# A place of its own for local attention's result, and an earlier split of the output weights

## The chip, the cores and the metric

The kernel runs on one core of a Trainium2 chip. The metric is the device time of one execution in microseconds, as the median of several executions. A core has five engines that run their own instruction streams and wait for each other by semaphores: TensorE (PE, matrix products; PEld is its loading of weights), VectorE (DVE), ScalarE (ACT), GpSimd (POOL) and SyncE (SP), which here issues nearly all transfers (DMA).

## The reference

Two attentions over the same input `x` (2048 rows, 448 columns, 16 heads of 28) are computed and mixed by a gate of each row:

```python
g = sigmoid((x * gate_w).sum(-1, keepdims=True))
# A: local; row s sees rows s, s-2, ..., s-14 (8 of them), masked below row 0
#    softmax over the 8 logits, then @ A_wo
# B: all 2048 rows; softmax(q k^T * 28**-0.5) v, then @ B_wo
out = g * A(x) + (1 - g) * B(x)
```

## The kernel before, in words

**Stages.** First come the projections to q, k and v of both attentions. Then follows a main loop of 256 steps, `st = 16 u + kt`: 16 units `u` (a group of four heads g = u // 4 and a block of 512 queries b = u % 4) times 16 tiles `kt` of 128 keys. A step computes the scores of four heads (L1039, twelve products into three PSUM tiles T), two exponentials on ACT (L1042) and, for the step before, the products with V into `av` (L993). Since the softmax of full attention needs the maxima of its rows beforehand, PE also computes up to three score tiles a step for a later unit (`s1_mm`, L144), and DVE reduces them (`s1_max`, L148). These run ahead, and the last ones are in step 234; then `s1_close` frees their PSUM banks for the output product.

**What runs beside the loop.** Local attention is done by POOL and DVE, in eight columns `c` of two heads: products with k, reductions, softmax, products with v (`a_av`, L664 and L669 into `oat`). A column's result, `oats[c % 2]`, is turned by DVE (`a_turn`, L675, into `oatT`) and stored to `oa_scr` in DRAM (`a_store`, L681, eight DMAs). These pieces stand in four lists (pool, dve, act, sp) with costs and needed lags in steps; `issue` takes from each list what fits into a step. Other work is put at a step and a place in it by `at(place, step, f)`, with the places pre, mid, dve, act and end in that order. Each engine's program order is the order in which the steps write its instructions; nothing is reordered at run time, so an instruction that waits holds back everything behind it on its engine. SP's DMAs wait in the same way.

**The end of a unit.** When unit u is through, in step 16(u + 1) + 1 its `av` is copied by ACT (`fin_copy`, L849, `osb`). Its sums go to DRAM and back (`fin_sum`, `fin_sum2`, L854 and L858), DVE takes reciprocals and POOL multiplies them by one minus the gate (`fin_inv`, L862 and L863, `finv`), SP stores them (`fin_spread`, L867) and loads them back broadcast (`fin_spread2`, L872, `rbc`). POOL multiplies (`fin_on`, L901), ACT and POOL split into a high and a low part (`fin_hi` L905, `fin_lo` L909), and SP stores both (`fin_store`, L101). For unit 13 these are at the steps 225, 226, 230 (reciprocal and store), 231, 233, 236, 237 and 239; for unit 12 fin_lo is in step 224 and fin_store in step 227.

**The output product.** It has seven chunks of 128 rows: the 448 rows of local attention (chunks 0 to 2 and half of 3), then the 448 of full attention. Every product is done in three terms of high and low parts (`op_mm`, L833). Its weights `wo` are loaded raw into `rawt` in steps 200 and 202, and split by POOL (`split_wo`, L774 and L775, once per chunk). The tiles of `wo` get the place of local attention's tiles: `load_wo` closes those pools and opens new ones, and the first write into the new tiles waits for all that still reads or writes the old ones. `a_done` does it once all four lists are empty, which is so in step 225; the splits are put at the steps 226 to 229. Then the turned rows of block 0 are loaded into `rawt` (`op_load_a(0)`, L795, step 230) and split (`op_split`, L806 to L809: the high part of block 0 on DVE, of other blocks on ACT, the low part on DVE). The high and low rows of full attention come from DRAM (`op_load_b`, tiles `on`).

The output product goes through a queue of 92 items (`op_queue`): for row tiles j = 0 to 7 seven chunks and a copy out, for j = 8 to 11 six chunks and a copy of the partial sum (`part`). From step `OPS[0]` on, each step takes five of them. OPS is set in step 234 to `st + 3`, step 237. When tile j = 4b + 2 begins, the rows of block b + 1 are split. What is left is done after the loop, together with unit 15's end.

Of the kernel before, what the change touches and what calls it, by code (L numbers as in the profile page):

```python
# [8 lines left out]
F32 = mybir.dt.float32  # L9
F32R = mybir.dt.float32r  # L10
AF = mybir.ActivationFunctionType
ALU = mybir.AluOpType
# [3 lines left out]
S, D, H, DH = 2048, 448, 16, 28  # L16
NB, NJ, NG = 4, 16, 4
# [8 lines left out]
def gated_mix_kernel(ctx: ExitStack, tc: tile.TileContext, xT, xn, gw, wA, wB, woAB, out):  # L26
    nc = tc.nc
# [51 lines left out]
    QP = [[cp.tile([128, 512], F32R, name=f"QP{i}{k}") for k in range(2)] for i in range(2)]  # L79
# [126 lines left out]
    with tc.tile_pool(name="xp", bufs=1) as xp, tc.tile_pool(name="wp", bufs=2) as wp:  # L206
# [203 lines left out]
        r, t = xst[:, 0, 0:3, :], xst[:, 0, 3, :]  # L410
# [7 lines left out]
        for kt in range(3):  # L418
            nc.vector.tensor_tensor(out=xl[0][:, kt, :], in0=r[:, kt, :], in1=xh[0][:, kt, :].bitcast(F32),
                                    op=ALU.subtract)  # L420
        nc.vector.tensor_tensor(out=tail[64:128], in0=t[64:128], in1=tail[64:128].bitcast(F32), op=ALU.subtract)
        nc.vector.tensor_tensor(out=wl0[:, 3, 0:256], in0=wt0[:, 0:256], in1=wh0[:, 3, 0:256].bitcast(F32),
                                op=ALU.subtract)
# [27 lines left out]
        for n, t in enumerate(tiles):  # L451
# [4 lines left out]
            for w in splits:  # L456
                i, k = (n - splits[w][0]) * splits[w][1], splits[w][1]
# [36 lines left out]
            if parts and parts[0][0] <= n:  # L494
                _, u, t = parts.pop(0)
# [4 lines left out]
            if n == 64:  # L500
                gate = []
                for sgn, dst in ((-1.0, g_t), (1.0, omg)):
                    e = sp.tile([128, NJ], F32, name="ez")
# [5 lines left out]
            if n == 70:  # L509
                r = max_turn(omw)  # L510
# [10 lines left out]
    def at(pos, st, f):  # L521
        hooks.setdefault((st, pos), []).append(f)
# [12 lines left out]
    pool = ctx.enter_context(tc.tile_pool(name="psv", bufs=1, space=bass.MemoryType.PSUM))  # L535
# [38 lines left out]
    ep = ctx.enter_context(tc.tile_pool(name="ep", bufs=1))  # L574
# [9 lines left out]
        nc.gpsimd.memset(maskt[0:1, w, 0:DIL * w, :], -1e9 / SCALE)  # L584


    actx = ExitStack()
    a1 = actx.enter_context(tc.tile_pool(name="a1", bufs=1))
    a2 = actx.enter_context(tc.tile_pool(name="a2", bufs=2))
    a3 = actx.enter_context(tc.tile_pool(name="a3", bufs=5))  # L590
    kvt = {}
    oats = [a1.tile([128, NJ, 2, 32], F32, name=f"oat{i}") for i in range(2)]
    for t in oats:
        nc.gpsimd.memset(t, 0.0)  # L594
    for nme in ("k", "v"):
        for i in range(2):
            t = a1.tile([128, HALO + NJ, 56], F32, name=f"{nme}t{i}")
            kvt[nme, i] = t
    qt, Lt, oat, lst, prods = {}, {}, {}, {}, {}
# [69 lines left out]
            nc.gpsimd.tensor_tensor(out=oat[c], in0=oat[c], in1=oat[c, w], op=ALU.add)  # L669

    def a_turn(c, i):
        if i == 0:
            oaTt[c] = a1.tile([128, NJ, 2, 32], F32, name="oatT")
        r = slice(4 * i, 4 * i + 4)
        nc.vector.transpose(oaTt[c][:, r].rearrange("p j h e -> p (j h e)"),  # L675
                            oats[c % 2][:, r].rearrange("p j h e -> p (j h e)"))

    def a_store(c, a):
        for h in range(2):
            f = 56 * c + DH * h  # L680
            nc.sync.dma_start(oa_scr[f:f + DH].rearrange("f (j p) -> f j p", j=NJ)[:, :, 32 * a:32 * a + 32],  # L681
                              oaTt[c][32 * a:32 * a + DH, :, h, :])

    oaTt = {}


    lists = {"pool": [], "dve": [], "act": [], "sp": []}
# [84 lines left out]
    def split_wo(k):  # L772
        raw = rawt[:, D * k:D * k + D]
        nc.gpsimd.tensor_copy(wo[0][:, k, :], raw)  # L774
        nc.gpsimd.tensor_tensor(out=wo[1][:, k, :], in0=raw, in1=wo[0][:, k, :].bitcast(F32), op=ALU.subtract)  # L775
# [4 lines left out]
    def a_done(st):  # L780
        adone.append(st)
        load_wo()

        for i, k in enumerate((4, 5, 6, 0, 1, 2, 3)):
            at("act", st + 1 + i // 2, lambda k=k: split_wo(k))
        at("end", st + 5, lambda: op_load_a(0))

    oaT, onT = {}, {}

    def op_load_a(b):  # L790
        cs = slice(512 * b, 512 * b + 512)
        for k in range(4):
            n = 128 if k < 3 else 64
            raws[b, k] = rawt[0:n, 512 * k:512 * k + 512]
            nc.sync.dma_start(raws[b, k], oa_scr[128 * k:128 * k + n, cs])  # L795

    def op_split(b, k):
        if k < 3:
            i = (6 * b + 2 * k) % 12
            oaT[b, k] = [spare[x // 4][:, 512 * (x % 4):512 * (x % 4) + 512] for x in (i, i + 1)]  # L800
        else:
            oaT[b, k] = on_tiles(b)[0]
        raw = raws.pop((b, k))
        hi, lo = (t[0:128 if k < 3 else 64, :] for t in oaT[b, k])
        if b:
            nc.scalar.activation(hi, raw, AF.Copy)  # L806
        else:
            nc.vector.tensor_copy(hi, raw)
        nc.vector.tensor_tensor(out=lo, in0=raw, in1=hi.bitcast(F32), op=ALU.subtract)  # L809

    raws = {}
    spare = KH[1], KH[2], KL[0]
# [1 line left out]
    def on_tiles(b):  # L814
        if b not in onT:
            onT[b] = [[oP["2"].tile([128, 512], F32R, tag=f"on{p}{k}", name=f"on{p}{k}") for p in ("hi", "lo")]
                      for k in range(4)]
        return onT[b]

    def op_load_b(b, k, rows=128):  # L820
# [7 lines left out]
    def op_mm(j, bank, ks, first=False, last=False):  # L828
        b, jj = divmod(j, 4)
        for k in ks:  # L830
            for i, (a, c) in enumerate(TERMS):
                src = (oaT[b, k] if k < 3 else onT[b][k - 3])[a][:, 128 * jj:128 * jj + 128]
                writes(bank, nc.tensor.matmul(bank[:, :D], src, wo[c][:, k, :],  # L833
                                              start=(first and k == ks[0] and i == 0),
                                              stop=(last and k == ks[-1] and i == 2)))

    def op_out(j, bank, eng=0):
        t = mtile("res")
        if eng:
            reads(bank, nc.vector.tensor_copy(t[:, :D], bank[:, :D]))  # L840
        else:
            reads(bank, nc.scalar.activation(t[:, :D], bank[:, :D], AF.Copy))
        nc.sync.dma_start(out.rearrange("(p j) c -> p j c", j=NJ)[:, j, :], t[:, :D])
# [103 lines left out]


    def op_part(j, bank):
        part[j] = oP["1"].tile([128, D], F32, name=f"part{j}")  # L950
        reads(bank, nc.scalar.activation(part[j], bank[:, :D], AF.Copy))

    def op_rest(j, bank):
# [7 lines left out]
    def op_queue(j):  # L961
        bank = accs[j % 2]
        b = j // 4
        if j == 0:
            ks = (4, 5, 6, 0, 1, 2, 3)
            return [(0, lambda k=k: op_mm(j, bank, (k,), first=k == 4, last=k == 3)) for k in ks] + [
                (0, lambda: op_out(j, bank))]
        return [
            (0, lambda: op_mm(j, bank, (0,), first=True)),
            (0, lambda: op_mm(j, bank, (1,))),  # L970
            (0, lambda: op_mm(j, bank, (2,))),
            (READY[b, 0], lambda: op_mm(j, bank, (3,))),
            (READY[b, 1], lambda: op_mm(j, bank, (4,))),
            (READY[b, 2], lambda: op_mm(j, bank, (5,), last=b == 2)),
        ] + ([(0, lambda: op_part(j, bank))] if b == 2 else [
            (READY[b, 3], lambda: op_mm(j, bank, (6,), last=True)),
            (0, lambda: op_out(j, bank)),
        ])
# [97 lines left out]
    for u in range(NU):  # L1076
        g, b = divmod(u, NB)
        for kt in range(NJ):
            st = NJ * u + kt
            if kt == (8 if u < 12 else 12) and u + 1 < NU:  # L1080
                load_q(u + 1)
            run("pre", st)
            issue("sp", st, 0)
            if st >= A_START:
                issue("pool", st, 4.2)
            if not adone and not any(lists.values()):
                a_done(st)
            cur = {}
            left = s1e - s1c[0]
            for a in scores(u, kt, cur):  # L1090
                if a == 2:
                    run("mid", st)
            run("dve", st)
            if u and kt == 6:
                late["dve"] += 0.25
            if finished:
                v = finished.pop(0)
                t = max_parts(v)
                late["dve"] += 0.3
                late["pool"] += 0.18  # L1100
                turned = {}
                lag = 2 if v < NU - 1 else 1
                at("dve", st + lag, lambda t=t, w=turned: w.update(r=max_turn(t.bitcast(F32))))
                at("end", st + lag, lambda v=v, w=turned: max_store(v, w["r"]))
            issue("dve", st, DLIM)
            issue("act", st, 0)
            run("act", st)
            if prev is not None:
                do_av(prev)
            else:  # L1110
                for _ in range(2):
                    nc.tensor.matmul(av, KH[0][:, 0:128], KH[0][:, 0:512], start=True, stop=True, skip_group_check=True)
            prev = (kt, cur, g)
            if OPS and st >= OPS[0]:
                op_some(st, 5)
            run("end", st)
            step = 2.25 if left else 2.1
            late["dve"] = max(0.0, late["dve"] + 0.58 * min(3, left) - step)
            late["pool"] = max(0.0, late["pool"] - step)
            if st == OP0 + 31:  # L1120
                op_load_b(2, 3)
            if not OPS and s1c[0] == s1e:
                s1_close()
                for k in range(4):
                    at("act", st + 1 + k // 2, lambda k=k: op_split(0, k))
                OPS.append(st + 3)
    do_av(prev)
    fin_copy(15)
    while opj[0] < 12 or opq:
# [52 lines left out]
```

## Time and profile before

| | |
|---|---|
| median of 3 runs | 915.58 us (914.75 to 916.93) |
| the profiled execution | 915.27 us, its span 913.4 us |
| busy: PE, DVE, ACT, POOL | 900.1, 740.7, 645.9, 626.4 us |
| mean granted TensorE clock | 0.996 |
| POOL's seven splits of the output weights | first at 772.1 us, 0.56 + 1.15 us each |
| first product of the output (L833) | 799.6 us |

A profile's span runs from the first to the last instruction; the execution's own time has 1.9 us around it. In rows of the timeline the columns are start (us from the span's start), duration, engine, line, operation, what is written from what, and in brackets the idle time of the engine just before and what ended it. A row with a count merges several instructions, and its duration is from the first start to the last end.

### The profile page before, as it was taken

What the parts mean: (1) busy time and instruction counts of PE and PEld (TensorE: products, weight loads), DVE (VectorE), ACT (ScalarE), POOL (GpSimd) and SP (SyncE); (2) the same over time, 40 slices, a digit from 0 to 9 for tenths busy, and PEclk for the clock granted to TensorE, in tenths of its full rate; (3) what the DMA queues carried; (4) which work ended last, traced back from release to release, by engine and by line L of the source; (5) the groups of instructions that cost most, each with busy time, mean ns of one, the idle gap of its engine ahead of it and who ended that gap; (6) DMA issues with size and microseconds to landing.
All of it is one profiled execution on the core that took longest, in us unless ns stands there. A gap on an engine that the chain in (4) does not pass through costs nothing.

```text
span 913.4 us, 20598 instructions
## 1 busy us (share of the span) xinstructions
PE 900.1 (99%) x8334; PEld 530.2 (58%) x8334; DVE 740.7 (81%) x997; ACT 645.9 (71%) x775; POOL 626.4 (69%) x494
## 2 busy tenths in 40 slices
PE   9999999999999999999999999999999999799998
PEld 6889999999944444444444444444444444266667
DVE  6488999999989998999999999999999988510112
ACT  6456434343378888888988888888989888644550
POOL 2499846564479799998989999899998294400100
PEclk9999999999999999999999999999999999899999
DMA  9977403554373331344244322522222422454323
GB/s 266 295 258 201 129 11 94 156 128 113 82 244 94 94 99 45 93 104 120 46 120 123 101 82 58 131 90 63 73 57 63 108 50 40 144 176 130 96 91 102
DMA packets 113839, 104.30 MB, mean 114 GB/s; under 512 B 74628, under 2 KB 82180, under 8 KB 112960
## 3 DMA queue, kind: packets, MB, share of 16 engines
q1 hardware_dynamic: 113600, 102.72, 39.3%
q8 instruction: 65, 1.06, 0.5%
q10 hardware_dynamic: 144, 0.26, 0.1%
q14 instruction: 30, 0.25, 0.1%
HBM read 61.99 MB, written 40.48 MB: 112 GB/s over the span
## 4 chain that ended last, share of the span: by engine, by line
PE 94%; ACT 2%; POOL 2%; DMA 1%; SPq 1%; DVE 1%; issue 0%; ACTq 0%; POOLq 0%; DVEq 0%
PE T L1039 29%; PE av L993 27%; PE r L298 15%; PE T L833 8%; PE r L293 7%; PE r L144 4%; PE T L144 4%; ACT P L1042 1%; POOL wo L775 1%; DMA V<-in_xT 1%; DMA rbc<-rs 0%; POOL wo L774 0%; DVE MX L148 0%; SPq L795 0%; POOL oat L594 0%
## 5 line engine op out<-in xcount | busy, mean ns | idle before, releaser
L1042 ACT ACTIVATE P<-T 128x1024 f32<-128x1024 f32 x512 | 497.4, 1025 | 96.1 <-PE T L1039 94.3
L148 DVE TENSOR_REDUCE MX<-T 128x1 f32<-128x512 f32 x470 | 440.3, 952 | 22.4 <-PE T L144 10.3
L993 PE MATMUL av<-P,V 128*32 128x512 f32 x2048 | 273.6, 606 | 1.1 <-ACT osb L849 0.8
L1039 PEld LDWEIGHTS T<-QH,KH 30*128 30x128 f32 x1024 | 91.1, 182 | 228.1 <-ACT P L1042 205.4
L144 PE MATMUL T<-KH,QP 28*128 28x512 f32 x704 | 219.4, 454 | 0.3 <-DVE MX L162 0.3
L1039 PE MATMUL T<-QH,KH 30*128 30x512 f32 x1024 | 212.2, 490 | 6.2 <-ACT P L1042 5.8
L162 DVE TENSOR_REDUCE MX<-r 128x2 f32<-128x1024 f32 x160 | 192.6, 1221 | 24.7 <-PE r L144 23.1
L1039 PE MATMUL T<-QH,KL 28*128 28x512 f32 x1024 | 186.5, 397 | 0.0
L1039 PE MATMUL T<-QL,KH 28*128 28x512 f32 x1024 | 184.0, 394 | 0.0
L615 POOL TENSOR_TENSOR prod<-qt,kt 128x896 f32<-128x896 f32 x64 | 135.2, 2115 | 0.2
L362 ACT ACTIVATE raw<-r 128x896 f32<-128x896 f32 (+1 forms) x64 | 58.9, 921 | 97.9 <-PE r L298 96.6
L669 POOL TENSOR_TENSOR oat<-oat,prod 128x896 f32<-128x896 f32 x56 | 118.2, 2111 | 2.7
L144 PEld LDWEIGHTS T<-KH,QP 28*128 28x128 f32 x704 | 86.0, 181 | 27.7 <-ACT P L1042 21.4
L664 POOL TENSOR_TENSOR prod<-vt,L 128x896 f32<-128x896 f32 x56 | 95.5, 1705 | 0.5
L363 POOL TENSOR_TENSOR ast<-raw 128x448 f32<-128x448 f32 x48 | 55.4, 1155 | 58.1 <-ACT raw L362 45.7
L1039 PEld LDWEIGHTS T<-QL,KH 28*128 28x128 f32 x1024 | 93.6, 185 | 0.0
L1039 PEld LDWEIGHTS T<-QH,KL 28*128 28x128 f32 x1024 | 92.4, 183 | 1.0
L993 PEld LDWEIGHTS av<-P,V 128*32 128x32 f32 x2048 | 40.3, 108 | 79.1 <-issue 72.5
L298 PE MATMUL r<-wh,xh 64*128 64x448 f32 (+1 forms) x512 | 83.5, 362 | 0.0
L144 PE MATMUL r<-KH,QP 64*128 64x512 f32 x320 | 83.1, 390 | 0.0
L298 PE MATMUL r<-wh,xl 64*128 64x448 f32 (+1 forms) x384 | 69.4, 363 | 0.0
L298 PE MATMUL r<-wl,xh 64*128 64x448 f32 (+1 forms) x448 | 64.8, 367 | 0.0
(116 smaller groups left out, 1031.7 us busy)
## 6 DMA issues: line engine op xcount, KB each, us to landing
a_scr<-ast SPq DMA_DIRECT2D x24, 448.0 KB
qk_hi<-qkh SPq DMA_DIRECT2D x24, 256.0 KB
qk_lo<-qkh SPq DMA_DIRECT2D x24, 256.0 KB
rbc<-rs SPq DMA_DIRECT2D x60, 64.0 KB
QP<-qk_hi SPq DMA_DIRECT2D x64, 56.0 KB
KL<-qk_lo SPq DMA_DIRECT2D x16, 224.0 KB
QH<-qk_hi SPq DMA_DIRECT2D x64, 56.0 KB
QL<-qk_lo SPq DMA_DIRECT2D x64, 56.0 KB
```

The source lines that it names most:

```text
L144: nc.tensor.matmul(bank, qhis[u][h % 2][r, 128 * qs:128 * qs + 128], KH[u // NB % 3][r, 512 * kc:512 * kc + 512], start=True, stop=True)
L148: r = nc.vector.tensor_reduce(MX[:, n % NMX:n % NMX + k], bank, axis=X, op=ALU.max)
L162: nc.vector.tensor_reduce(m, PM[k], axis=X, op=ALU.max)
L293: nc.tensor.matmul(bank, ws[c][rows, k, t[4]:t[4] + 128], x, start=first, stop=last)
L298: nc.tensor.matmul(bank[:, 0:cols], x, ws[c][rows, k, 0:cols], start=first, stop=last)
L615: nc.gpsimd.tensor_tensor(out=p, in0=qt[c], in1=kvt["k", c % 2][:, HALO - DIL * w:HALO - DIL * w + NJ, :], op=ALU.mult)
L664: nc.gpsimd.tensor_tensor(out=dst, in0=kvt["v", c % 2][:, HALO - DIL * w:HALO - DIL * w + NJ, :].rearrange("p j (h d) -> p j h d", d=DH), ...
L669: nc.gpsimd.tensor_tensor(out=oat[c], in0=oat[c], in1=oat[c, w], op=ALU.add)
L833: writes(bank, nc.tensor.matmul(bank[:, :D], src, wo[c][:, k, :], start=(first and k == ks[0] and i == 0), stop=(last and k == ks[-1] and ...
L993: nc.tensor.matmul(av[32 * h:32 * h + 32, :], V[:, kt, 4 * g + h, :], tiles_[h], start=(kt == 0), stop=(kt == NJ - 1), skip_group_check=True)
L1039: nc.tensor.matmul(bank[a], (KH[g % 3], KH[g % 3], KL[g % 2])[t][r, ks], (qh, ql, qh)[t][r, :], start=(t == 0), stop=(t == 2))
L1042: e = nc.scalar.activation(p, RP[0] if a == "2" else mine, AF.Exp, scale=SCALE).ins
```

## The change

`oats` and `oatT` move from a pool of local attention to the pool `ep`, which stays open. `a_done` is now called when POOL's list alone is empty, in step 221, and one chunk of the weights is split in each of the steps 221 to 227, in the order 0 to 6. When all lists are empty, in step 225, a new function `a_stored` puts `op_load_a(0)` at step 229 and the splits of block 0's turned rows at the steps 232, 232, 233 and 234. For block 0 both halves of that split are now POOL's. The output queue starts two steps after the last row maximum (step 236), and its first tile takes the chunks in the order 0 to 6 like the others. The fourth pair of `on` tiles is now the pair `QP[b % 2]` of the row-maximum products, and the partial sums of tiles 8 to 11 lie in `oats`.

```diff
+    oats = [ep.tile([128, NJ, 2, 32], F32, name=f"oat{i}") for i in range(2)]
+    oatT = ep.tile([128, NJ, 2, 32], F32, name="oatT")
+    for t in oats:
+        nc.gpsimd.memset(t, 0.0)
...
-    oats = [a1.tile([128, NJ, 2, 32], F32, name=f"oat{i}") for i in range(2)]
-    for t in oats:
-        nc.gpsimd.memset(t, 0.0)
...
     def a_turn(c, i):
-        if i == 0:
-            oaTt[c] = a1.tile([128, NJ, 2, 32], F32, name="oatT")
...
-        for i, k in enumerate((4, 5, 6, 0, 1, 2, 3)):
-            at("act", st + 1 + i // 2, lambda k=k: split_wo(k))
-        at("end", st + 5, lambda: op_load_a(0))
+        for k in range(7):
+            at("act", st + k, lambda k=k: split_wo(k))
+
+    def a_stored(st):
+        adone.append(st)
+        at("end", st + 4, lambda: op_load_a(0))
+        for k, i in enumerate((7, 7, 8, 9)):
+            at("act", st + i, lambda k=k: op_split(0, k))
...
-            nc.vector.tensor_copy(hi, raw)
-        nc.vector.tensor_tensor(out=lo, in0=raw, in1=hi.bitcast(F32), op=ALU.subtract)
+            nc.gpsimd.tensor_copy(hi, raw)
+        (nc.vector if b else nc.gpsimd).tensor_tensor(out=lo, in0=raw, in1=hi.bitcast(F32), op=ALU.subtract)
...
-                      for k in range(4)]
+                      for k in range(3)] + [QP[b % 2]]
...
-        part[j] = oP["1"].tile([128, D], F32, name=f"part{j}")
+        i = (j - 8) % 2 * D
+        part[j] = oats[(j - 8) // 2].rearrange("p j h e -> p (j h e)")[:, i:i + D]
...
-        if j == 0:
-            ks = (4, 5, 6, 0, 1, 2, 3)
-            return [(0, lambda k=k: op_mm(j, bank, (k,), first=k == 4, last=k == 3)) for k in ks] + [
-                (0, lambda: op_out(j, bank))]
...
-            if not adone and not any(lists.values()):
+            if not adone and not lists["pool"]:
                 a_done(st)
+            if len(adone) == 1 and not any(lists.values()):
+                a_stored(st)
...
-                for k in range(4):
-                    at("act", st + 1 + k // 2, lambda k=k: op_split(0, k))
-                OPS.append(st + 3)
+                OPS.append(st + 2)
```

More of the change, by code (lines that the diff above doesn't have):

```diff
@@ L671, in a_turn @@
     def a_turn(c, i):
-        if i == 0:
-            oaTt[c] = a1.tile([128, NJ, 2, 32], F32, name="oatT")
         r = slice(4 * i, 4 * i + 4)
-        nc.vector.transpose(oaTt[c][:, r].rearrange("p j h e -> p (j h e)"),
+        nc.vector.transpose(oatT[:, r].rearrange("p j h e -> p (j h e)"),
                             oats[c % 2][:, r].rearrange("p j h e -> p (j h e)"))
@@ L681, in a_store @@
             nc.sync.dma_start(oa_scr[f:f + DH].rearrange("f (j p) -> f j p", j=NJ)[:, :, 32 * a:32 * a + 32],
-                              oaTt[c][32 * a:32 * a + DH, :, h, :])
-    oaTt = {}
+                              oatT[32 * a:32 * a + DH, :, h, :])
     lists = {"pool": [], "dve": [], "act": [], "sp": []}
```

## The prediction

> **What bounds the kernel now.** The page first, then a table of stretches over the last fifth, where everything that the change touches lies.
>
> ```profile
> PE 900.1 (99%) x8334; PEld 530.2 (58%) x8334; DVE 740.7 (81%) x997; ACT 645.9 (71%) x775; POOL 626.4 (69%) x494
> ```
> ```profile
> 780.00:785.00 5.00, 5.00 (x53) 1.85 (x45) 4.36 (x6) 4.31 (x6) 4.26 (x6) 1.00 0.00 0
> 785.00:790.10 5.10, 4.54 (x44) 1.49 (x40) 0.21 (x1) 3.06 (x5) 0.00 (x0) 1.00 0.76 220
> 790.10:795.20 5.10, 0.00 (x0) 0.00 (x0) 1.36 (x3) 1.58 (x3) 2.31 (x3) 0.90 0.85 241
> 795.20:801.10 5.90, 5.76 (x24) 2.72 (x25) 4.01 (x7) 2.82 (x3) 0.39 (x1) 0.50 0.56 180
> 803.50:820.00 16.50, 16.03 (x120) 9.71 (x119) 2.49 (x4) 10.22 (x15) 0.00 (x0) 1.00 0.67 203
> 820.00:840.00 20.00, 20.00 (x140) 12.89 (x137) 0.25 (x1) 10.23 (x13) 0.22 (x1) 1.00 0.46 131
> ```
>
> The page says that TensorE (PE) is busy for 99% of the span, so only PE's holes are for the taking. The columns of the table are the stretch, its length, then PE, PEld, DVE, ACT and POOL with counts, the granted clock, the DMA share and GB/s. PE is full up to 785 and again from 820; between them lies the one large hole, 5.1 us with no matmul at all (790.1 to 795.2), and behind it 5.9 us at a granted clock of 0.50. The DMA column of the first row is 0.00: for those 5 us nothing moves, though loads are wanted. Since PE is full again behind the hole (20.00 of 20.00), what is gained in it is carried to the end.
>
> The chain of waits and the timeline of that place show why (the step is st = 16u + kt; L849 of step 225 starts at 763.29 and L905 of step 236 at 793.62, which fixes the steps between).
>
> ```profile
> 772.09 0.56 POOL L774 CAST wo<-rawt 128x448 fp32r<-128x448 f32 x1 [11.50 <-DVE MX L148]
> ...
> 783.09 1.15 POOL L775 TENSOR_TENSOR wo<-rawt,wo 128x448 fp32r<-128x448 f32 x1
> 784.19 0.23 POOL L863 TENSOR_TENSOR finv<-finv,og 128x16 f32<-128x16 f32 x1
> 792.33 1.26 POOL L901 TENSOR_TENSOR on<-osb,rbc 128x512 f32<-128x512 f32 x1 [7.91 <-DMA rbc<-rs]
> ```
> ```profile
> 763.31 7.11 SPq L681 DMA_DIRECT2D oa_scr<-oatT  x8
> 770.52 0.56 SPq L854 DMA_DIRECT2D rs<-osb  x1
> 772.28 0.36 SPq L858 DMA_DIRECT2D fsum<-rs  x1
> ...
> 774.48 1.61 SPq L101 DMA_DIRECT2D on_lo<-onlo  x4
> 784.45 0.34 SPq L867 DMA_DIRECT2D rs<-finv  x1
> 784.83 1.93 SPq L795 DMA_DIRECT2D rawt<-oa_scr  x4
> 786.87 1.91 SPq L872 DMA_DIRECT2D rbc<-rs  x4
> ```
> ```profile
> 763.29 0.60 ACT L849 ACTIVATE osb<-av 128x512 f32<-128x512 f32 x1
> ...
> 793.62 0.63 ACT L905 ACTIVATE onhi<-on 128x512 fp32r<-128x512 f32 x1 [5.56 <-POOL on L901]
> 794.16 1.92 ACT L1042 ACTIVATE P<-T 128x1024 f32<-128x1024 f32 x2
> ```
>
> Read from the bottom: the exponentials of step 236 (794.16) stand on ACT behind fin_hi (L905), which waits for Pool's fin_on (L901), which waits for the broadcast of the reciprocals (rbc), which SP issues at 786.87 behind the store at 784.45, which waits for Pool's little product L863 at 784.19. That product has its input ready long before, and stands behind the seven splits of the output weights, 772.09 to 784.24. The splits start so late because wo lies in the place of oats and oatT: its first writer waits for the last oatT store (issued up to 770.42). "DVE MX" in the bracket had nothing to do with it.
>
> **The change part by part.**
>
> *Own place for oats and oatT; splits from step 221 on.* The tiles move to a pool that stays open, so wo no longer waits for the turns and stores. Pool's last local-attention instruction is the first row here:
>
> ```profile
> 756.24 2.10 POOL L669 TENSOR_TENSOR oat<-oat,prod 128x896 f32<-128x896 f32 x1
> 759.31 1.28 POOL L909 TENSOR_TENSOR onlo<-on,onhi 128x512 fp32r<-128x512 f32 x1 [0.96 <-ACT onhi L905]
> ```
> ```profile
> 776.36 0.24 DVE L862 RECIPROCAL finv<-fsum 128x16 f32<-128x16 f32 x1
> ```
>
> Same seven splits, same price: (784.24 - 772.09) / 7 = 1.74 us each. They now run from 758.3; the four of steps 221 to 224 pass before fin_lo (L909), which moves from 759.3 to 765.3 and ends at 766.6. Its reader, the on_lo store, is issued only at 774.48, behind the oatT stores, so this costs nothing. The other three end at 771.8. L863 then follows its reciprocal at once: 776.9 in place of 784.4.
>
> *SP's queue.* op_load_a(0) moves from step 230 to 229, past the reciprocal's store. SP is free at 776.1 (end of the on_lo stores): rows 776.1 to 778.0, the store at 778.4. Until that store has landed rbc cannot be issued. Lower bound: 1.76 us, as rs<-osb to fsum (770.52 to 772.28), so 780.2. Upper: behind the rows in the same engines.
>
> ```profile
> rawt<-oa_scr SPq DMA_DIRECT2D x12, 256.0 KB
> ```
>
> The rows are three of these and half a one, 896 KB, at 220 GB/s 4.2 us, so 776.1 + 1.8 + 4.2 = 782.1 and, with the store, 782.5. I take the upper end: in the run of before rbc, issued behind rows, landed 3.5 us after its last issue (788.78 to 792.33). So rbc goes out 782.5 to 784.4 and lands between 786.2 (1.8 us) and 787.9 (3.5 us); with the rows landed by then, 786.2. [...] Without queueing rbc would be in at 784 and rival 3 below would lose its ground; the sum would stay.
>
> *The turned rows split by Pool, not DVE.* On DVE a split was 0.41 + 0.69 us; Pool's cast for 512 columns is 0.558 x 512/448 = 0.64 and its subtraction is L909's shape, 1.28: with gaps 1.95.
>
> ```profile
> L774 POOL CAST wo<-rawt x7: 555/558/560, 772.1 to 782.5; 128x448 fp32r<-128x448 f32 x7
> L808 DVE CAST KH<-rawt x3: 385/414/418, 793.9 to 797.1; 128x512 fp32r<-128x512 f32 x3
> L809 DVE TENSOR_TENSOR KH<-rawt,KH x8: 685/692/1783, 794.4 to 875.1; 128x512 fp32r<-128x512 f32 x8
> ```
>
> First row in at 776.1 + 3.5 = 779.6 (3.5 as rbc above); three splits to 785.5; fin_on 786.2 to 787.5; the nmt product 0.22; fourth split to 789.7. DVE has nothing else to do there. So fin_hi ends at 788.1 and the exponentials of step 236 go when their scores are done, about 789, not at 794.16.
>
> *Output product from step 236 (was 237), in order 0 to 6.* PE's prices:
>
> ```profile
> 799.65 3.94 PE T L833 x15
> ...
> 808.12 0.91 PE T L1039 x9
> 809.03 0.99 PE av L993 x8
> 810.02 3.24 PE T L833 x15
> ```
> ```profile
> 789.01 1.07 PE L993 MATMUL av<-P,V 128*32 128x512 f32 x8
> ```
>
> In step 236 PE is done with av at 790.08 and now has 15 matmuls of output product, 3.24 us, to 793.3. They need row chunk 3 at 792.0 (Pool done 789.7, slack 2.3) and the B chunks: SP issues those behind rbc; 1.84 MB at 241 GB/s is 7.6 us from 786.2 on, 256 KB for chunk 3 first (787.3), then 512 KB each (789.4, 791.6, 793.8), wanted at 792.0, 792.7, 795.2 and 795.9. All hidden, by 2 us or more. The next scores start at 793.3, when their banks are long free.
>
> *Sum.* Before, from 790.08 to 803.59 (next scores after the first 15 products) PE should need 0.91 + 0.99 + 3.24 = 5.14 and took 13.5: 8.3 lost (5.1 empty, 2.95 by half clock over 5.9 us, 0.3 in small gaps). All of it goes.
> A second, small hole goes too: in step 240 ACT had an output copy, four row splits and the osb copy in a row, and av waited for osb.
>
> ```profile
> 818.64 0.49 ACT osb L849
> 819.18 1.06 PE av L993 x8
> ```
>
> PE was short of 16.50 - 16.03 = 0.47 in that stretch; one step earlier, the splits and osb fall into different steps: 0.4 gained. Paid back at the end: 92 queue items at five a step filled steps 237 to 254 and two of 255; now two of 254 and none of 255, so the last step has nothing to cover its exponentials.
>
> ```profile
> 884.83 0.51 PE L1039 MATMUL T<-QH,KH 30*128 30x512 f32 x4
> 885.85 1.94 ACT L1042 ACTIVATE P<-T 128x1024 f32<-128x1024 f32 x2 [3.21 <-PE T L1039]
> 887.84 1.06 PE L993 MATMUL av<-P,V 128*32 128x512 f32 x8 [0.24 <-ACT P L1042]
> ```
>
> Scores at T let the exponentials run T+1.0 to T+3.0; the last scores, eight of twelve of them waiting for that bank, finish some 0.7 later (8/12 of 0.91, and a start), the last exponentials at T+5.7. PE has 0.91 + 0.99 + 0.65 + 0.91 + 0.99 = 4.5 us of work in that time: 1.2 idle against the 0.24 above, so 0.9 lost. Net 8.3 + 0.4 - 0.9 = 7.8.
> *At nothing:* QP in place of a fourth on pair (its last reader is a row-maximum product, and unit 14's are over some twenty steps before the first load into it); part in oats (last read by the turns, over twenty steps earlier); the earlier K, V tiles of local attention 4 KB higher, behind Pool's memsets at the loop's start, bounded by a microsecond either way off PE.
>
> The profiled execution took 915.27 (span 913.4), 0.3 under the median 915.58. 915.27 - 7.8 = 907.5; on the median, **907.8**.
>
> **The rivals.**
> 1. *A shorter hole stays.* If loads run slower than 220 GB/s (the stretch from 795.2 shows 180), the B chunks come in at 786.2 + 10.2 = 796.4 for the last one, and Pool's rows and rbc later as well; PE then waits 1 to 3 us in steps 236 and 237: 909 to 911. For it: DMA is 0.76 to 0.85 busy in the hole. Against: those loads now spread over the empty 780 to 785. [...]
> 2. *The splits do not move*: something else still holds wo's new place until 772.1. Then fin_lo ends at 780.3, its store and the rows follow, rows from 783.7, rbc in at 793.8, the fourth row split at 797.3: a hole of 5.3 plus 2.95 against the 7.8: 916, no change. Against: the other tiles of that place are read by Pool itself or long before 756.
> 3. *Slower.* fin_on now stands on Pool between the third and fourth row split, and rbc behind the rows. With fin_on's end at E, the fourth split ends at E + 2.2 and PE idles from E = 789.8 on; with 2.95 for the clock the 7.8 are used up at E = 794.6, rbc landing 7.2 us later than I reckon. At 10 us late it is 7.7 + 2.95 lost, 918.4. Against: rbc landed 5.5 us after its first issue even behind rows.
>
> **How the numbers follow.** Forecast 0.75 (own range 906.8 to 909.2: the end loss 0.4 to 1.3, the small gaps kept or not, the runs' spread), rival 1 0.13, rival 2 0.05, rival 3 0.04, the rest 0.03 anywhere. The range reaches over half of rival 1: 906.5 to 910.5. About 0.2% (1.8 us) is what this kernel's measurement can tell: faster 0.75 + 0.13 + 0.01 = 0.89, same 0.06, slower 0.05.
>
> **What would show it.** Right: L774 first at about 758.4; L863 at about 776.7; rows issued at about 776, rbc about 782.5; Pool row splits 779.6 to 789.7; no stretch with PE empty for over 1 us between 785 and 885, granted clock 1.00 throughout; first L833 at about 790.1. Wrong: L774 still near 772; a PE wait on a DMA of onhi or onlo or on Pool's row split at step 236; ACT's L905 held past 790; a hole late in the tail (885 to 905) longer than 2 us.

## The result, and the profile after

The changed kernel takes 908.34 us (four runs, 908.00 to 908.42) where the kernel before takes 915.54 (four runs on the same chip, 914.75 to 916.93): a ratio of 0.9919 with a 95% interval of 0.9902 to 0.9936, or 7.2 us less; 907.8 was predicted. The profiled execution is one of 908.42 us with a span of 906.3.

The stretches around the old hole and at the end, in the kernel after; the columns are the stretch, its length, then PE, PEld, DVE, ACT and POOL with counts, the granted clock, the DMA share and GB/s:

```profile
785.00:790.10 5.10, 4.58 (x44) 1.49 (x40) 1.04 (x3) 4.76 (x8) 3.80 (x5) 1.00 0.55 180
790.10:795.20 5.10, 5.10 (x39) 3.39 (x35) 0.00 (x0) 1.69 (x3) 1.59 (x2) 1.00 0.73 232
795.20:801.10 5.90, 5.90 (x44) 3.52 (x37) 0.00 (x0) 3.86 (x5) 0.00 (x0) 1.00 0.29 84
801.10:820.00 18.90, 18.90 (x133) 12.03 (x132) 2.49 (x4) 10.84 (x16) 0.00 (x0) 1.00 0.65 206
876.00:883.00 7.00, 6.19 (x47) 2.62 (x40) 0.52 (x1) 4.64 (x6) 0.00 (x0) 1.00 0.00 0
```

The stretch that had no matmul at all (790.1 to 795.2) is full, the one behind it has its full clock, and step 240's small hole is gone too (18.90 of 18.90). What is left is half a microsecond in 785 to 790, which the kernel before has as well, and a new 0.81 in 876 to 883: the last steps have lost their cover.

The timelines of POOL, SP, ACT and PE in the kernel after show how it comes about:

```profile
758.91 0.55 POOL L772 CAST wo<-rawt 128x448 fp32r<-128x448 f32 x1
...
765.83 1.29 POOL L912 TENSOR_TENSOR onlo<-on,onhi 128x512 fp32r<-128x512 f32 x1
...
777.32 0.22 POOL L866 TENSOR_TENSOR finv<-finv,og 128x16 f32<-128x16 f32 x1 [5.02 <-DVE finv L865]
780.05 0.61 POOL L811 CAST KH<-rawt 128x512 fp32r<-128x512 f32 x1 [2.51 <-PE T L1039]
787.08 1.28 POOL L904 TENSOR_TENSOR on<-osb,rbc 128x512 f32<-128x512 f32 x1 [1.22 <-DMA rbc<-rs]
789.17 1.27 POOL L812 TENSOR_TENSOR onlo<-rawt,onhi 64x512 fp32r<-64x512 f32 x1
```
```profile
776.70 1.93 SPq L798 DMA_DIRECT2D rawt<-oa_scr  x4
778.72 0.53 SPq L870 DMA_DIRECT2D rs<-finv  x1
783.66 1.71 SPq L875 DMA_DIRECT2D rbc<-rs  x4
```
```profile
763.91 0.61 ACT L852 ACTIVATE osb<-av 128x512 f32<-128x512 f32 x1
...
788.63 0.63 ACT L908 ACTIVATE onhi<-on 128x512 fp32r<-128x512 f32 x1
789.59 1.94 ACT L1042 ACTIVATE P<-T 128x1024 f32<-128x1024 f32 x2 [0.33 <-PE T L1039]
```
```profile
790.69 2.09 PE L836 MATMUL T<-wo,KH 128*128 128x448 f32 x9
...
793.92 0.51 PE L1039 MATMUL T<-QH,KH 30*128 30x512 f32 x4
```

In the changed kernel the lines from L795 to L909 of the kernel before are numbered three higher (L849 is L852, L905 is L908), L774 and L775 are L772 and L773, and the loop's L993, L1039 and L1042 keep their numbers; the kernels of the experiments shift by a few lines again. The splits of the weights run from 758.91 to 772.3, the little product L866 follows its reciprocal at 777.32, and the exponentials of step 236 go at 789.59, waiting 0.33 us for their scores and for nothing else. The 15 output products and the next scores take 790.69 to 793.92, 3.23 us.

The last unit's osb copy is the mark at the far end, first in the kernel before, then in the kernel after:

```profile
889.04 0.60 ACT L849 ACTIVATE osb<-av 128x512 f32<-128x512 f32 x1 [0.81 <-PE av L993]
```
```profile
881.70 0.60 ACT L852 ACTIVATE osb<-av 128x512 f32<-128x512 f32 x1 [1.25 <-PE av L993]
```

It comes 7.3 us earlier. The first mark, unit 13's osb, is at 763.91 against 763.29: the changed kernel comes to the place 0.6 us late. So between the two marks 7.96 us were gained (117.79 in place of 125.75).

### The profile page after: what moved, and what is told of

Its sections match the earlier page's. It is cut to its first block, busy times and chain, and to the rows that moved or that the text cites. A ratio compares the mean times of both kernels' runs of the same rounds, so it can differ in the third digit from the quotient of the medians.

```text
span 906.3 us, 20587 instructions
## 1 busy us (share of the span) xinstructions
PE 898.3 (99%) x8334; PEld 531.4 (59%) x8334; DVE 735.0 (81%) x989; ACT 646.1 (71%) x775; POOL 634.1 (70%) x502
## 4 chain that ended last, share of the span: by engine, by line
PE 97%; ACT 1%; DMA 1%; DVE 0%; POOL 0%; issue 0%; SPq 0%; ACTq 0%; DVEq 0%; POOLq 0%
PE T L1039 30%; PE av L993 28%; PE r L298 15%; PE T L836 8%; PE r L293 7%; PE r L144 4%; PE T L144 4%; ACT P L1042 1%; DMA V<-in_xT 1%; POOL oat L590 0%; DVE MX L148 0%; DVE MX L162 0%; ACT osb L852 0%; ACT wh L214 0%; ACT L L642 0%
## 5 line engine op out<-in xcount | busy, mean ns | idle before, releaser
L1042 ACT ACTIVATE P<-T 128x1024 f32<-128x1024 f32 x512 | 497.4, 1025 | 93.6 <-PE T L1039 91.6
L993 PE MATMUL av<-P,V 128*32 128x512 f32 x2048 | 272.7, 605 | 1.2 <-ACT P L1042 0.8
L1039 PEld LDWEIGHTS T<-QH,KH 30*128 30x128 f32 x1024 | 90.9, 181 | 222.4 <-ACT P L1042 198.7
L1039 PE MATMUL T<-QH,KH 30*128 30x512 f32 x1024 | 211.8, 489 | 0.9 <-ACT P L1042 0.6
L1039 PE MATMUL T<-QH,KL 28*128 28x512 f32 x1024 | 186.2, 397 | 0.0
L1039 PE MATMUL T<-QL,KH 28*128 28x512 f32 x1024 | 183.7, 393 | 0.0
L1039 PEld LDWEIGHTS T<-QL,KH 28*128 28x128 f32 x1024 | 93.5, 184 | 0.0
L1039 PEld LDWEIGHTS T<-QH,KL 28*128 28x128 f32 x1024 | 92.1, 183 | 1.0
L993 PEld LDWEIGHTS av<-P,V 128*32 128x32 f32 x2048 | 40.3, 108 | 79.6 <-issue 72.6
L144 PE MATMUL r<-KH,QP 64*128 64x512 f32 x320 | 80.2, 390 | 0.0
L298 PEld LDWEIGHTS r<-wh,xh 64*128 64x128 f32 x512 | 63.6, 185 | 1.2
```

Of the source, the lines that this page charges most:

```text
L144: nc.tensor.matmul(bank, qhis[u][h % 2][r, 128 * qs:128 * qs + 128], KH[u // NB % 3][r, 512 * kc:512 * kc + 512], start=True, stop=True)
L298: nc.tensor.matmul(bank[:, 0:cols], x, ws[c][rows, k, 0:cols], start=first, stop=last)
L993: nc.tensor.matmul(av[32 * h:32 * h + 32, :], V[:, kt, 4 * g + h, :], tiles_[h], start=(kt == 0), stop=(kt == NJ - 1), skip_group_check=True)
L1039: nc.tensor.matmul(bank[a], (KH[g % 3], KH[g % 3], KL[g % 2])[t][r, ks], (qh, ql, qh)[t][r, :], start=(t == 0), stop=(t == 2))
L1042: e = nc.scalar.activation(p, RP[0] if a == "2" else mine, AF.Exp, scale=SCALE).ins
```

## The experiments

Each ratio is against runs of the kernel before that were measured beside the experiment. The profiled execution is one of the runs, and its rows belong to its own time.

**The place alone.** The kernel before with oats and oatT in `ep`, and with the two moves of memory (QP, the partial sums) that make the room; splits, rows and the start of the queue as before.

```diff
+    oats = [ep.tile([128, NJ, 2, 32], F32, name=f"oat{i}") for i in range(2)]
+    oatT = ep.tile([128, NJ, 2, 32], F32, name="oatT")
...
-                      for k in range(4)]
+                      for k in range(3)] + [QP[b % 2]]
...
-        part[j] = oP["1"].tile([128, D], F32, name=f"part{j}")
+        part[j] = oats[(j - 8) // 2].rearrange("p j h e -> p (j h e)")[:, i:i + D]
```

> The kernel before with only the own place for oats and oatT (and, so that all fits, the fourth on pair in QP and the partial sums in oats); the splits of the weights keep their old steps 226 to 229, the turned rows stay on DVE, the output queue starts in step 237 and its first tile keeps its order. My theory: the place alone is the lever, since Pool waits for nothing else; the splits run from about 760.6 to 772.8 us, L863 at about 776.7, fin_on at about 785, scores of step 238 at about 796 in place of 803.6; no end loss, nothing gained in step 240: 915.5 - 7.6 = 907.9, as fast as the whole change within 0.5. Rival (the early steps 221 to 227, Pool's row splits and the start in step 236 each carry a part): 909.5 to 912.

Measured: 908.68 (908.16 to 908.93) against 915.38, ratio 0.9923 (0.9908 to 0.9937): 6.7 of the 7.2 us, which the intervals do not tell from the whole. It is 0.8 above the expected 907.9 and below the rival's range. In its POOL timeline and its stretches:

```profile
761.02 0.56 POOL L773 CAST wo<-rawt 128x448 fp32r<-128x448 f32 x1
```
```profile
790.00:795.00 5.00, 4.61 (x36) 2.38 (x29) 2.87 (x4) 3.34 (x4) 0.88 (x1) 1.00 0.44 142
805.00:820.00 15.00, 14.53 (x102) 9.28 (x101) 2.74 (x5) 9.22 (x13) 0.00 (x0) 1.00 0.46 129
```

The splits start at 761.02 though they still stand in the steps 226 to 229: where they stand orders Pool's program and sets no time. It was the release of the place that held them until 772.09. Step 240's hole is still there (0.47 short in 805 to 820), as it should be with the old start of the queue.

**The wait put back.** The changed kernel with the splits behind a memset of oatT, called once all lists are empty, so that Pool waits again for the last oatT store; the rest of the change stands.

```diff
-            if not adone and not lists["pool"]:
+            if not adone and not any(lists.values()):
...
+        at("act", st, lambda: nc.gpsimd.memset(oatT, 0.0))
         for k in range(7):
-            at("act", st + k, lambda k=k: split_wo(k))
+            at("act", st + k // 2, lambda k=k: split_wo(k))
```

> The changed kernel with the old wait put back by itself: the splits again in steps 225 to 228, and ahead of them a Pool memset of oatT, which must wait for the last oatT store to have read it. All else as changed. My theory: splits from about 773.4 to 785.6 us, rows issued behind the fifth split at about 782, rbc landed at about 794, fin_on to 795.3, the fourth row split done at 797.5 where PE wants it at 792: a hole of 5.5 us plus 2.95 at half clock: 908.3 + 8.4 = 916.7, no better than before. Rival (the order of the steps carries the gain, not the wait): 908.5 to 910.

Measured: 910.15 (910.08 to 911.38) against 915.38, ratio 0.9943 (0.9928 to 0.9957). A miss: 5.2 of the 7.2 us stay although the wait is there. POOL, SP and PE of this run:

```profile
773.54 0.95 POOL L782 MEMSET oatT<- 128x1024 f32 x1 [11.49 <-DMA oa_scr<-oatT]
...
786.57 0.22 POOL L867 TENSOR_TENSOR finv<-finv,og 128x16 f32<-128x16 f32 x1
```
```profile
777.98 5.70 SPq L799 DMA_DIRECT2D rawt<-oa_scr  x4
```
```profile
794.57 0.67 PE L837 MATMUL T<-wo,onhi 128*128 128x448 f32 x2 [0.86 <-POOL onhi L812]
795.92 0.47 PE L837 MATMUL T<-wo,onlo 128*128 128x448 f32 x1 [0.67 <-POOL onlo L813]
```

The wait is there: Pool waits 11.49 us and starts 1.56 us behind the last of the oatT stores' issues (771.98), in the kernel before 1.67 behind its last (770.42). L867 is 9 us late, as meant. What failed is my reckoning of what follows. The rows' loads go out one by one as the splits free `rawt` (5.70 us for four), and their last issue is 3.1 us ahead of the store's (786.81), so rbc goes out at 788.27, 1.5 us behind the store, and Pool's fin_on ends at 793.79, against 788.36 (0.9 of that is there at unit 13's osb, 764.84 against 763.91). And in step 236 PE has nine products of chunks 0 to 2 to do, which need only the rows. So PE waits 0.86 and 0.67 us, and the clock stays at 1.00. This profile is of the slowest of the four runs, 911.38; the other three took 910.08 to 910.22. The rest of the change thus gains 5.2 us in spite of the wait, the place alone 6.7, both 7.2: they are two ways to the same hole, not two gains. Which of the rest's parts (the earlier start of the queue, Pool's rows, the rows' loads ahead of the store) carry the 5.2 us no run separates.

**The rows split by DVE.** Block 0's row splits back on DVE, at the same steps.

```diff
-            nc.gpsimd.tensor_copy(hi, raw)
-        (nc.vector if b else nc.gpsimd).tensor_tensor(
+            nc.vector.tensor_copy(hi, raw)
+        nc.vector.tensor_tensor(
```

> The changed kernel with block 0's turned rows split by DVE again, at the same steps 232 to 234. My theory: DVE is nearly full with the row maxima until step 234 (about 0.25 us free in each step), so 3 x 1.1 us of row splits push the last maxima 2 to 2.9 us back and PE's scores with them, of which the hole of 0.5 us before 790 takes a part: 908.3 + 2.2 = 910.5 (909.5 to 911.3). Rival (the engine does not matter, DVE is the faster one and has time): 908.3 within 0.4.

Measured: 910.9 (910.07 to 911.0) against 915.38, ratio 0.9946 (0.9931 to 0.996). DVE's and PE's timelines of this run:

```profile
782.14 0.42 DVE L811 CAST KH<-rawt 128x512 fp32r<-128x512 f32 x1
...
784.26 1.82 DVE L148 TENSOR_REDUCE MX<-T 128x1 f32<-128x512 f32 x2
...
787.06 1.28 DVE L148 TENSOR_REDUCE MX<-T 128x1 f32<-128x512 f32 x2
```
```profile
785.00 0.50 PE L144 MATMUL T<-KH,QP 28*128 28x512 f32 x1 [0.34 <-DVE MX L148]
786.13 0.50 PE L1039 MATMUL T<-QH,KH 30*128 30x512 f32 x2 [0.63 <-DVE MX L148]
```

Two splits (782.14 to 784.34) stand ahead of the last pair but one of the row maxima, a third (786.00 to 787.14) ahead of the last pair, and PE waits 0.34 and 0.63 us for banks that these maxima free. The first output product comes at 793.08 in place of 790.69; 0.6 of these 2.4 us are there at unit 13's osb already (764.50), before the edit's place. So the earlier steps for the rows cost nothing because they are Pool's. The time is the expected one (910.5, range 909.5 to 911.3).

**The rows behind the store.** `op_load_a(0)` one step later, so that SP issues the reciprocal's store first.

```diff
-        at("end", st + 4, lambda: op_load_a(0))
+        at("end", st + 5, lambda: op_load_a(0))
```

> The changed kernel with the load of the turned rows one step later, so that the small store of the reciprocals goes out ahead of the rows, as before. My theory: the store lands within 1.8 us, rbc goes out at about 780 in place of 783.7 and lands at about 784.5 behind the rows; the rows come 1.2 us later, the third row split ends at about 787.3, fin_on at 788.6 and the fourth split at 790.9, inside the slack of about 2 us: no change, 908.3 within 0.4. Rival (rbc behind the rows costs PE time): 907.5 or less.

Measured: 908.2 (907.6 to 908.35) against 915.38, ratio 0.9916 (0.9899 to 0.9933): no change of time. SP of this run:

```profile
777.85 0.34 SPq L870 DMA_DIRECT2D rs<-finv  x1
778.23 2.96 SPq L798 DMA_DIRECT2D rawt<-oa_scr  x4
781.38 1.82 SPq L875 DMA_DIRECT2D rbc<-rs  x4
```

Ahead of the rows, the 8 KB store is through by 3.5 us at most, when SP has issued the rows; behind them it takes 4.9 us (778.72 to 783.66, in the rows of after). Since rbc 2.3 us earlier brings nothing, neither order sets the time.

**How late may fin_on be?** Two, four, six and eight memsets of oatT (128x1024, nothing reads it any more) on POOL right ahead of unit 13's fin_on: rival 3 made by hand.

```diff
+        if u == 13:
+            for _ in range(n):
+                at("end", f + l[4], lambda: nc.gpsimd.memset(oatT, 0.0))
         at("end", f + l[4], lambda u=u: pool_time(1.24, fin_on, u, fin["r"]))
```

> The changed kernel with two memsets of oatT (0.92 us each, 1.8 us together) on Pool ahead of unit 13's fin_on. The fourth row split then ends at 792.3 us; PE wants it at 792.6. My theory: hidden, 908.3 within 0.4. Rival (the chain over fin_on and ACT is what PE waits for already): 910.1.

> As the run before with four memsets, 3.7 us. My theory: the slack of 2.2 us goes first, a hole of 1.5 us is left on PE in step 236 and the clock stays whole: 909.8. Rival (any hole halves the clock): 912.7.

> As before with six memsets, 5.5 us. A hole of 3.3 us: 911.6 if it is too short to lower the clock, up to 914.6 if it lowers it as the hole of 5.1 us in the kernel before did. [...]

> As before with eight memsets, 7.4 us. A hole of 5.2 us and 2.95 at half clock: 916.5, which is the break-even of my third rival (fin_on ending about 7 us late). Rival (only the hole counts, the clock recovers at once): 913.5.

Measured, against 916.24 for the kernel before (the first row against 916.18, beside the next experiment); the 95% intervals follow the ratios, and the last two columns are of the profiled executions:

| memsets | time us | ratio | their time us | fin_on ends |
|---|---|---|---|---|
| 0 (the changed kernel again) | 908.33 | 0.9917 (0.9904 to 0.9929) | | 788.60 |
| 2 | 908.32 | 0.9918 (0.9903 to 0.9932) | 1.96 | 789.20 |
| 4 | 908.9 | 0.9926 (0.9909 to 0.9943) | 3.98 | 791.24 |
| 6 | 912.89 | 0.997 (0.9958 to 0.9982) | 6.00 | 794.22 |
| 8 | 915.31 | 0.9987 (0.9978 to 0.9996) | 8.02 | 795.65 |

The waits of PE with four, six and eight memsets, from the three timelines:

```profile
793.38 0.47 PE L836 MATMUL T<-wo,onlo 128*128 128x448 f32 x1 [0.49 <-POOL onlo L812]
```
```profile
795.00 0.86 PE L836 MATMUL T<-wo,onhi 128*128 128x448 f32 x2 [1.83 <-POOL onhi L811]
796.35 0.74 PE L836 MATMUL T<-wo,onlo 128*128 128x448 f32 x1 [0.49 <-POOL onlo L812]
```
```profile
796.43 1.12 PE L836 MATMUL T<-wo,onhi 128*128 128x448 f32 x2 [4.04 <-POOL onhi L811]
797.78 0.74 PE L836 MATMUL T<-wo,onlo 128*128 128x448 f32 x1 [0.23 <-POOL onlo L812]
```

And the stretches around those waits, for six and for eight:

```profile
790.00:795.00 5.00, 3.17 (x19) 1.77 (x17) 0.21 (x1) 0.74 (x2) 4.81 (x6) 1.00 0.73 256
795.00:800.00 5.00, 4.51 (x22) 2.50 (x26) 0.00 (x0) 1.88 (x3) 2.50 (x2) 0.53 0.20 53
800.00:805.00 5.00, 5.00 (x28) 2.88 (x24) 0.00 (x0) 2.32 (x3) 0.00 (x0) 0.78 0.47 131
```
```profile
790.00:795.00 5.00, 2.39 (x13) 1.61 (x9) 0.00 (x0) 0.00 (x0) 4.77 (x6) 0.96 0.65 216
795.00:800.00 5.00, 3.34 (x10) 2.11 (x14) 0.21 (x1) 2.46 (x3) 3.88 (x5) 0.50 0.13 28
800.00:805.00 5.00, 5.00 (x36) 2.87 (x32) 0.00 (x0) 2.49 (x3) 0.00 (x0) 0.85 0.28 92
```

The first memset or so only fills the 1.22 us that Pool waited for rbc anyway, and two cost nothing, as expected. Four open a wait of 0.49 us, and the time grows by about as much (908.9 against 908.32; 909.8 was expected). With six and eight the price is more than the wait, and it lies between the two values that were named for each. In the profiled executions, from the first output product to the scores of step 238, the kernel after takes 7.77 us (790.69 to 798.46), the one with six memsets 13.39 (791.09 to 804.48) and the one with eight 14.60 (790.31 to 804.91). Of the 5.6 us that six add, 2.3 are waits (1.83 + 0.49) and 3.3 are the clock at half; of the 6.8 of eight, 4.3 and 2.6. The profiled execution with six is the slowest of its six runs (914.39, mean clock 0.996). The other five, 912.19 to 913.96, have one of 0.997 or 0.998, so there the clock took less, and the median 912.89 is 4.6 above that of two memsets.

Rival 1's 909 to 911 counts a hole of 1 to 3 us at its own length. With six memsets the granted clock is 1.00 in 790 to 795 and 0.53 in 795 to 800. In slices of 0.05 us the clock of the kernel before is 1.00 or 0.50 there, but for the two slices in which it changes; if it is so here too, the mean of 0.53 puts the fall at about 795.3. PE is at work again from 795.00, and the second wait (795.86 to 796.35) has not begun: in this profile the one wait of 1.83 us went ahead of the fall, so a hole of that length cost more than itself.

**The changed kernel again, and cover for the end.** The changed kernel was measured a second time, beside a kernel that takes four items a step from step 249 on, so that seven items instead of two are left for steps 254 and 255.

```diff
-                op_some(st, 5)
+                op_some(st, 5 if st < 249 else 4)
```

> The changed kernel itself, for the two runs beside it: 908.3.

> The changed kernel with four items of the output queue a step from step 249 on (five before that), so that steps 254 and 255 keep 4 and 3 items. My theory: the last exponentials are covered again, the 0.8 to 0.9 us of the end loss come back: 907.5. Rival (the end is set by unit 15's own chain, not by PE's work): 908.3.

Measured: the changed kernel 908.33 (908.12 to 908.87), ratio 0.9917 (0.9904 to 0.9929) against 916.18; with cover 907.09 (906.98 to 907.15), ratio 0.9902 (0.9889 to 0.9915). The stretch of the end in that run, to be set against the last row of after's stretches:

```profile
876.00:883.00 7.00, 7.00 (x48) 3.97 (x48) 1.23 (x3) 3.09 (x4) 0.00 (x0) 1.00 0.01 3
```

The 0.81 us are gone, and 1.24 are gained. In the kernel after the 0.81 are a wait of the last products with V for ACT's last exponentials:

```profile
878.63 1.06 PE L993 MATMUL av<-P,V 128*32 128x512 f32 x8
880.51 1.06 PE L993 MATMUL av<-P,V 128*32 128x512 f32 x8 [0.81 <-ACT P L1042]
```

The stretch table shows only a part of the loss, since PE counts as busy while the scores ahead of it go slowly: from the first of them to the next products with V it is 1.22 us there (877.41 to 878.63), and 0.91 in the kernel before (884.83 to 885.74). So the loss was 1.1 us. From unit 13's osb to the last unit's the cover brings 1.0 us (116.72 in place of 117.76), and 0.2 more lie behind the last osb (24.4 in place of 24.6).

**The queue from step 235.** The half microsecond that PE lacks in 785 to 790 might be filled with output products one step earlier (three in step 235, five a step to 244, then four).

```diff
-                op_some(st, 5)
+                op_some(st, 3 if st == OPS[0] else 5 if st < 245 else 4)
...
-                OPS.append(st + 2)
+                OPS.append(st + 1)
```

> As the run before, and the queue starts in step 235 with three items (chunks 0 to 2, whose rows Pool has split by then), five a step to 244 and four after. My theory: PE's hole of 0.5 us between 785 and 790 is filled too: 907.0. Rival (the third chunk's rows or the banks are not free in time and PE waits as long elsewhere): 907.5.

Measured: 910.19 (907.55 to 911.32, six runs), ratio 0.9932 (0.9918 to 0.9946) against 916.18: four of the six runs lie above all runs of the changed kernel measured beside it (908.12 to 908.87), and the median misses both expectations. PE's waits and two stretches of it:

```profile
794.06 0.68 PE L836 MATMUL T<-wo,onhi 128*128 128x448 f32 x2 [1.17 <-DMA onhi<-on_hi]
795.50 0.68 PE L836 MATMUL T<-wo,QP 128*128 128x448 f32 x2 [0.25 <-DMA QP<-on_hi]
```
```profile
785.00:790.00 5.00, 5.00 (x45) 2.72 (x41) 0.86 (x3) 4.03 (x7) 4.27 (x5) 1.00 0.62 197
795.00:800.00 5.00, 4.56 (x24) 1.53 (x23) 0.00 (x0) 2.02 (x3) 0.00 (x0) 0.66 0.40 118
```

The hole in 785 to 790 is filled, and the next one opened: the full-attention chunks are now wanted before their loads land, and the waits lowered the clock to 0.66 in 795 to 800. The two lowest of the six runs (907.55 and 908.71) have a mean clock of 1.000 over the span, the other four (909.91 to 911.32) one of 0.996 to 0.998. So the slack of the transfers behind rbc, about 2 us by the prediction, was used up, and what the filled hole brought went into the new waits even where the clock stayed whole (907.55 against 907.09 with the cover alone). The start in step 235 also draws the load of block 1's rows forward (issued at 789.25, in the kernel after at 799.88), behind the chunks' loads in the same queue; what it adds to their lateness no run separates.

**Together.** The changed kernel with the store first, three items in step 235, two in step 236, then five, and four from step 249 on: an earlier start that asks for the late chunks no sooner.

```diff
-        at("end", st + 4, lambda: op_load_a(0))
+        at("end", st + 5, lambda: op_load_a(0))
...
-                op_some(st, 5)
+                op_some(st, {235: 3, 236: 2}.get(st, 5 if st < 249 else 4))
...
-                OPS.append(st + 2)
+                OPS.append(st + 1)
```

> The changed kernel with three things: the end cover of e6 (four items a step from 249 on), the small store ahead of the turned rows (as e4, so rbc and the B chunks go out about 2 us earlier), and the queue's first five items taken as three in step 235 and two in step 236, so that no chunk is wanted earlier than its load lands, which is what the start in step 235 of e7 got wrong. My theory: e6's 907.1 less the 0.5 us hole before 790, clock whole: 906.5. Rival (a chunk still comes late, or the hole cannot be filled, since the scores of step 236 move back by as much): 907.1, and up to 910 where a late chunk lowers the clock as in e7.

Measured: 905.93 (905.54 to 906.0) against 915.83, ratio 0.9889 (0.9872 to 0.9905): the best version, 9.9 us under the kernel before. One stretch over the whole of the output product's part, in which PE is busy for 96.73 us in the kernel before:

```profile
780.00:883.00 103.00, 103.00 (x747) 62.35 (x744) 15.07 (x26) 60.86 (x78) 12.86 (x14) 1.00 0.47 141
```

The expectation was 906.5, 0.6 more. It had counted the hole before 790 by the stretch table, as 0.5 us. By the rows it was larger: the scores of step 236 take 1.82 us up to the next products with V in the second profile of the changed kernel (787.80 to 789.62), and 0.91 here (789.73 to 790.64). By the table PE has no hole left in this stretch, so little more is to be had there by moving work beside it.

## Why the prediction was right, and where its sizes were off

- *The cause of the hole.* Shown: with the place alone the splits start at once and 6.7 us are gained. That the place is what Pool waits for is shown both ways, since with the wait alone put back Pool waits 11.49 us for the oatT store. That the wait must cost the time is not so: put back, it costs 1.8 of the 7.2 us, because the rest of the change hides most of it. The prediction gave the parts one common sum and did not say what each is worth alone. Rival 2 (something else holds the place) fell.
- *Rival 1.* It did not come about: PE waits for no load there, and it is busy without a gap from 790.10 to 820 in the stretches of the kernel after. Its 909 to 911 counts a hole of 1 to 3 us at its own length alone, an estimate of mine that no run shows: waits of 0.86 and 0.67 us went by with the clock at 1.00 (the wait put back), one wait of 1.83 us was followed by 0.53 in 795 to 800 (six memsets).
- *Pool's splits, fin_lo, L863.* 758.91, 765.83 and 777.32 against the reckoned 758.4, 765.3 and 776.7: each 0.5 to 0.6 late, as the changed kernel is at unit 13's osb.
- *SP's queue.* Rows at 776.70 (776.1), store at 778.72 (778.4), rbc at 783.66 (782.5). Taking the upper end, behind the rows, was right; the run with the store first shows the other order. Of the 1.2 us that rbc is late, 0.6 are the late arrival; that rbc came 0.6 later still was in the slack.
- *Pool's rows.* 780.05 to 790.44 against 779.6 to 789.7; fin_on at 787.08 against 786.2. Durations held (0.61 for the cast, 1.28 for the product).
- *The 8.3 of the hole, the 0.4 of step 240, the 0.9 of the end.* From the end of the products with V in step 236, output products, scores and the next products with V take 5.14 us (790.69 to 795.83), as reckoned, where the kernel before took 13.5. Step 240's stretch is full. At the end 1.1 us are lost (1.2 reckoned), 0.9 net of the 0.24 of the kernel before. From unit 13's osb to the last unit's the gain is 7.96 us, against 7.8 in the sum.
- *What the sum did not have.* 0.6 us are lost before the place. The thirteen profiles of kernels with the own place have unit 13's osb between 763.59 and 764.84, the one profile of the kernel before at 763.29; of the 0.6, 0.2 stand at unit 0 already (292.67 against 292.49) and 0.3 come between the osb copies of units 11 and 12 (691.07 to 727.64 against 690.78 to 727.06). The prediction had allowed a microsecond either way for the earlier tiles' new places and taken nothing. Whether it is these places, or the spread of executions, no run here separates. Another 0.2 us are lost behind the last osb (24.60 us to the end of the span, 24.36 before). So 7.96 - 0.62 - 0.24 gives the 7.1 us by which the two spans differ (913.4 and 906.3).
- *A premise that did not hold.* "DVE has nothing else to do there" left the last row maxima out, which DVE reduces up to 785.6 in the kernel after. It did no harm, because the rows went to Pool; with the rows on DVE the time is 910.9 in place of 908.3.
- *Rival 3's break-even.* Reckoned with fin_on 7.1 us late (ending at 794.6 in place of 787.5); 7.3 us late (795.65 in place of 788.36) the kernel is still 0.1% under the one before. The slope was overdrawn because only the high half of chunk 3 is wanted first: the wait with eight memsets is for L811, 4.04 us, and the low half adds 0.23, while I had PE wait for both.

## What to carry to other kernels

When a late engine's work begins with a wait for a tile's place, the place is the thing to change: here an own place brought 6.7 of 7.2 us with the instructions where they were. Before adding up the parts of a change, ask for each alone which hole it closes; two parts that close the same one are worth little more than the larger (here 6.7 and 5.2 gave 7.2 together). And when work is drawn forward, look at which of its inputs has the least slack, and draw forward the rest.

## What the runs showed of the hardware that I had not expected

The granted clock of TensorE fell behind shorter waits than the 5.1 us of the kernel before. Behind one wait of 1.83 us (six memsets) it was 0.53 in 795 to 800. With the queue from step 235 (waits of 1.17 and 0.25 us in the rows above, and of 0.19 up to 796.37) it was 0.66 in 795 to 800 of the profiled run; two of the six runs have a mean clock of 1.000. With waits of 0.86 and 0.67 us (the wait put back) and of 0.49 (four memsets) it was 1.00 in every stretch from 790 to 805. In slices of 0.05 us, half clock lasts 6.8 us in the kernel before (794.22 to 801.05). Taken as 1.00 or 0.50 in the other profiles as well, the stretches give about 6.9 us with six memsets (0.53 and 0.78 in 795 to 805), about 6.9 with eight (0.96, 0.50 and 0.85 in 790 to 805), and 3.4 with the queue from step 235 (0.66 in 795 to 800, 1.00 in the stretches on both sides). The price on top of the waits is about half of the time that PE works in it: 2.95 us in the kernel before, 3.3 with six memsets, 2.6 with eight. What lowers the clock is not settled by these runs: the waits add up to 1.61 us in the run from step 235 and to 1.53 with the wait put back, where the clock stayed whole.
